# Sliding-window attention with a gated feed-forward: token tiles of 512 instead of 384 from the fifth tile on

## Chip, cores and metric

The kernel runs on one core of a Trainium2 chip. The metric is the time of one execution on the device, in microseconds (us). The median of three runs of the kernel before is given, and one further execution was profiled.

## What is computed

Attention over a window of 64 positions, causal, for 8 batches of 8 heads, 576 positions and 64 values a head; the heads' outputs side by side are the 512 features of 4608 tokens, and these go through a feed-forward layer with a ReLU gate (width 1536).

```python
scores = scale * np.matmul(q, k.transpose(0, 1, 3, 2))
rel = pos[:, None] - pos[None, :]
mask = (rel >= 0) & (rel < window)            # window = 64
attn = softmax(np.where(mask, scores, -1e9))
x = np.matmul(attn, v)      # (B, H, S, D) -> (B * S, H * D)
gate = np.maximum(x @ w_gate, 0.0)
out = gate * (x @ w_val) @ w_out
```

Inputs and output are fp32; the kernel computes in fp16 with fp32 accumulation.

## The kernel before, in words

Tokens are worked on in 12 tiles of `TT` = 384. A tile is two units of `U` = 192 tokens, and a unit is three windows of 64 queries; a batch has nine windows, or three units. For each tile there are two kinds of work.

Attention, by unit. The *scores* (`u_st`, L246) of four heads run beside each other in the four 32-row groups of TensorE, each head group into a bank of its own: 48 small matmuls, two pairs of banks of the pool `a_ps` (tag "a", two buffers of two banks). ScalarE takes the exponential bank by bank (`u_exp`, L257), VectorE multiplies by the band mask (`u_mask`, L265). The *values* (`u_pv`, L271) are 48 small matmuls, four beside each other by column groups, into one pair of banks; every query's sum of weights comes out as a 65th column. VectorE takes its reciprocal, multiplies (`u_recip`, `u_norm`) and transposes by 32x32 blocks into the feed-forward's input `xt` (`u_turn`, L315).

Feed-forward, by tile. `hidden` (L352): for each of 12 blocks of 128 features four matmuls with `w_gate` and four with `w_val`, each group into a bank of the pool `f_ps` (tag "h", four buffers of one bank); ScalarE writes the ReLU of the first to `r_sb`, VectorE multiplies it with the second into `g_sb` (L370). `output` (L410): for each 128 tokens 12 matmuls of 512 columns, a copy by ScalarE to `o_sb` (three buffers) and a store by the SyncE queue. The last block of the last tile (`output_last`, L419) is done in two column halves; the copy of the second half is split between ScalarE and VectorE, both into one `o_sb`.

The order on every engine is the order of the program, which is made when the kernel is built by a `Weaver` (L18): a heap of actions with due times and a clock in us that is advanced by an assumed cost for each group of matmuls. An action is put into the program when the clock has passed its time. `pair(t, TA, TB, P)` (L526) puts down the two score bursts, exponentials, masks, value bursts and transposes of tile t so that they fall into the feed-forward of tile t-1; `loads(t, T)` (L538) does the same for the loads of a batch's queries and keys, their transposes on VectorE (`qk_trans`, L175), and the values, which are loaded by the GpSimd queue (`v_load`, L182) and copied to the other half of the partitions by GpSimd (`v_spread`, L189). Before the loop over tiles all of this is put down at once, with T stepping by 25.4 from tile to tile:

```python
        T = 67.0
        for t in range(3, NU // 2):
            loads(t, T + 3.0)
            pair(t, T + 11.0, T + 14.0, T + 17.5)
            T += 25.4
```

`ready(n)` (L348) takes actions from the heap until the n-th unit has been transposed. The first two tiles have a schedule of their own.

Of the kernel before, what the change touches and what calls it, by code (L numbers as in the profile page):

```python
# [10 lines left out]
FP32 = mybir.dt.float32  # L11
FP16 = mybir.dt.float16
# [32 lines left out]
def kernel(  # L45
# [10 lines left out]
    nc = tc.nc  # L56
# [9 lines left out]
    G = 4  # L66
    scale = 1.0 / float(D) ** 0.5
    TT = 2 * U
    assert NT % TT == 0 and TT % 128 == 0

    consts = ctx.enter_context(tc.tile_pool(name="consts", bufs=1))
    persist = ctx.enter_context(tc.tile_pool(name="persist", bufs=1))
# [56 lines left out]

    def xt_tile(t):  # L130
        if t not in xts:
            xts[t] = x_sb.tile([128, NC, TT], FP16, name="xt")
        return xts[t]


# [46 lines left out]
    def v_load(u, parts=None):  # L182

        b, uu = divmod(u, UB)
        for g, lo, hi in parts or (((1, 0, 128), (3, 0, 128)), ((5, 0, 128),), ((7, 0, 128), (NG - 1, 64, 128)))[uu]:
            nc.gpsimd.dma_start(v16s[b % 2][lo:hi, g, :, 0:64],  # L186
                                v[b, :, 64 * g - 64 + lo:64 * g - 64 + hi].rearrange("h p d -> p h d"))

    def v_spread(u, copy=None, h0=0, h1=H):  # L189

        b, uu = divmod(u, UB)
        t = v16s[b % 2]
        copy = copy or nc.vector.tensor_copy
        for g0, g1 in (((0, 3),), ((4, 5),), ((6, 7),))[uu]:
            copy(t[64:128, g0:g1:2, h0:h1, 0:64], t[0:64, g0 + 1:g1 + 1:2, h0:h1, 0:64])  # L195
        for g0, g1 in (((2, 3),), ((4, 5),), ((6, 9),))[uu]:
            copy(t[0:64, g0:g1:2, h0:h1, 0:64], t[64:128, g0 - 1:g1 - 1:2, h0:h1, 0:64])  # L197
# [11 lines left out]
    def one_bank(name):  # L209
        return f_ps.tile([128, 512], FP32, name=name, tag="h")  # L210

    def two_banks(name):
        return a_ps.tile([128, 2, 512], FP32, name=name, tag="a")
# [10 lines left out]
    def st_block(to, g, hh, n, biased=False):  # L224

        b, w = divmod(n, NG)
        rows = slice(32 * g, 32 * g + 32)
        return [lambda dh=dh: nc.tensor.matmul(  # L228
            to, kTs[b % 2][rows, hh, 64 * w:64 * w + 128, dh], qTs[b % 2][rows, hh, 64 * w:64 * w + 64, dh],
            start=(dh == 0 and not biased), stop=(dh == 1), skip_group_check=biased) for dh in range(2)]  # L230

    def run_rows(rows):

        for step in zip(*rows):
            for dh in range(2):
                for block in step:
                    block[dh]()
# [77 lines left out]
    def u_turn(u, hhs=(0, 1)):  # L315

        d = units[u]
        c0 = U * (u % 2)
        h0, h1 = hhs[0], hhs[-1] + 1
        for hh in range(h0, h1):  # L320
            dst = xt_tile(u // 2)[:, 2 * hh:2 * hh + 2, c0:c0 + U].rearrange("p e (s c) -> p s e c", c=32)
            nc.vector.transpose(dst, d["x"][:, hh])  # L322
        if h1 == 2:
            del units[u]
            normed[0] = u + 1

    def plan_batch(b, load, trans):
        for i, (name, hh) in enumerate((n, hh) for n in "kq" for hh in range(2)):
            if load is not None:
                W.at(load, lambda name=name, hh=hh: qk_load(b, name, hh))  # L330
            W.at(trans[i], lambda name=name, hh=hh: qk_trans(b, name, hh))
# [16 lines left out]
    def ready(n):  # L348
        while normed[0] < n:
            W.pop()  # L350

    def hidden(t, spans, f0=0, f1=NF, each=1):  # L352

        if t not in gs:
            gs[t] = g_sb_p.tile([128, NF, TT], FP16, name="g_sb"), {}
        g_sb, done = gs[t]
        xt = xt_tile(t)
        n = spans[0][1] - spans[0][0]

        w = 512 // n  # L360
        each = max(each, w)

        def part(tile):
            return tile[:, 0:w * n].rearrange("p (w n) -> p w n", w=w)

        def relu(r_sb, h1):
            nc.scalar.activation(part(r_sb), part(h1), ACT.Relu)  # L367

        def gate(f, c0, r_sb, h2):
            nc.vector.tensor_tensor(g_sb[:, f:f + w, c0:c0 + n], part(r_sb), part(h2), MUL)  # L370
            done.update(dict.fromkeys(range(f, f + w), c0 + n))

        for fb in range(f0, f1, each):
            r_sbs = {}
            for i, wt in enumerate((wg, wv)):
                for c0, f in ((c0, f) for c0, _ in spans for f in range(fb, fb + each, w)):
                    h = f_ps.tile([128, 512], FP32, name=f"h{i}", tag="h")
                    for b in range(w):
                        W.advance(W.clock)
                        w_need(wt, f + b)  # L380
                        for c in range(NC):
                            nc.tensor.matmul(h[:, b * n:b * n + n], wt[:, c, (f + b) * 128:(f + b) * 128 + 128],  # L382
                                             xt[:, c, c0:c0 + n], start=(c == 0), stop=(c == NC - 1))
                        W.clock += 4 * (n + 7) / 2400.0
                    if i == 0:
                        r_sb = r_sbs[c0, f] = f_sb.tile([128, TT], FP32, name="r_sb", bufs=6)
                        W.at(W.clock, lambda r_sb=r_sb, h=h: relu(r_sb, h))
                    else:
                        W.at(W.clock, lambda f=f, c0=c0, r_sb=r_sbs[c0, f], h=h: gate(f, c0, r_sb, h))
# [10 lines left out]
    def out_evac(t, op, sub):  # L400
        def evac():
            o_sb = f_sb.tile([128, DM], FP32, name="o_sb")
            nc.scalar.copy(o_sb, op)  # L403
            nc.sync.dma_start(out[bass.ds(t * TT + sub * 128, 128)], o_sb)
        W.at(W.clock, evac)

    def op_tile():
        return f_ps.tile([128, DM], FP32, name="op", tag="h")

    def output(t, subs=range(TT // 128)):  # L410
        for sub in subs:
            op = op_tile()
            for f in range(NF):
                if f % 4 == 0:
                    W.advance(W.clock)
                out_mm(t, op, sub, f)
            out_evac(t, op, sub)

    def output_last(t):  # L419

        last = TT // 128 - 1
        output(t, range(last))
        W.drain()
        for col in range(2):
            op = op_tile()
            for f in range(NF):
                g_sb, _ = gs[t]
                nc.tensor.matmul(op[:, 0:256], g_sb[:, f, bass.ds(last * 128, 128)], wo[:, f, 256 * col:256 * col + 256],  # L428
                                 start=(f == 0), stop=(f == NF - 1))
            parts = ((0, 256, nc.scalar.copy, nc.sync),) if col == 0 else (  # L430
                (0, 128, nc.scalar.copy, nc.scalar), (128, 256, nc.vector.tensor_copy, nc.sync))
            o_sb = f_sb.tile([128, DM], FP32, name="o_sb")
            for c0, c1, copy, queue in parts:
                copy(o_sb[:, c0:c1], op[:, c0:c1])  # L434
                queue.dma_start(out[bass.ds(t * TT + last * 128, 128), 256 * col + c0:256 * col + c1], o_sb[:, c0:c1])

    def output_by_rows(t):
        ops = [op_tile() for _ in range(TT // 128)]
# [8 lines left out]
    with tc.manual_schedule():  # L447
# [78 lines left out]
        def pair(t, TA, TB, P):  # L526
            for u, T in ((2 * t, TA), (2 * t + 1, TB)):
                W.at(T, lambda u=u: u_st(u))
                plan_exps(T, u)
            W.at(P, lambda: u_pv(2 * t) + u_pv(2 * t + 1))  # L530
            for n in range(2):
                u = 2 * t + n
                W.at(P + 0.7 + 1.7 * n, lambda u=u: u_recip(u))
                for hh in range(2):
                    W.at(P + 0.9 + 0.5 * hh + 1.7 * n, lambda u=u, hh=hh: u_norm(u, hh))
                W.at(P + 1.9 + 1.7 * n, lambda u=u: u_turn(u))

        def loads(t, T):  # L538
            for u in (2 * t, 2 * t + 1):
                b, uu = divmod(u, UB)  # L540
                if uu == 0:
                    plan_batch(b, T - 12.0, (T, T + 1.4, T + 2.8, T + 4.2))
                W.at(T - 6.0, lambda u=u: v_load(u))
                W.at(T + 1.0, lambda u=u: v_spread(u, pool))

        for u in (4, 5):
            W.at(52.0, lambda u=u: v_spread(u, pool))
        pair(2, 56.0, 59.0, 62.5)
        T = 67.0
        for t in range(3, NU // 2):  # L550
            loads(t, T + 3.0)
            pair(t, T + 11.0, T + 14.0, T + 17.5)
            T += 25.4
        W.advance(15.3)
        hidden(0, ((0, U), (U, TT)), 0, 4, 4)
        hidden(0, ((0, TT),), 4, NF, 4)
        hidden(1, ((0, U),), each=4)
        output_by_rows(0)
        ready(4)
        hidden(1, ((U, TT),))  # L560
        output(1)
        for t in range(2, NU // 2):
            ready(2 * t + 2)
            hidden(t, ((0, TT),))
            (output if t < NU // 2 - 1 else output_last)(t)
        W.drain()


# [28 lines left out]
```

The softmax here doesn't subtract the row's maximum and nothing guards it: scores larger than these inputs give would overflow.

## Time and profile before

| | |
|---|---|
| median of 3 runs | 326.93 us (326.75 to 329.27) |
| the profiled execution | 326.75 us, span in the profile 325.1 us |
| mean granted TensorE clock | 0.989 |
| TensorE matmuls | 4043 recorded |
| hidden part of tile 2 (the third) begins | 67.81 |
| of tile 3 | 93.40 |
| of tile 4 | 118.99 |
| of tile 11 (the last) | 298.37 |
| last matmul ends | 321.78 |

The beginnings are read from the chain of waits in order of time, at the first hidden matmuls behind a tile's output matmuls. PE is TensorE's matmuls, PEld its weight loads, ACT is ScalarE, DVE VectorE, POOL GpSimd, SP SyncE. "L382" is line 382 of the kernel. In a list of groups `h<-xt,wg` names the tile written and those read; in brackets behind an instruction stand the engine's idle time before it and what ended it.

### The profile page before, as it was taken

The page shows a single profiled execution, that of the slowest core. Times are in us where ns is not written, and L with a number is a line of the kernel's source. Part 1 is how long each engine was busy: PE and PEld are TensorE (multiplying, and loading weights), DVE is VectorE, ACT ScalarE, POOL GpSimd, SP SyncE. Part 2 cuts the span into 40 slices and gives each one's busy share as a digit, 9 for nine tenths or more (in the row PEclk, how much of TensorE's full clock was granted, in tenths as well). Part 3 has the DMA queues.
Part 4 walks back from the last instruction along what each step waited for, and adds up shares of the span by engine and source line. Part 5 has one row for each costly group of instructions (what it writes and reads, how often), then busy time and mean ns, then how long its engine had stood idle before and what let it go on. Part 6 is the DMA issues. An engine that isn't in the chain of part 4 may idle for free.

```text
span 325.1 us, 9418 instructions
## 1 busy us (share of the span) xinstructions
PE 315.2 (97%) x4043; PEld 187.2 (58%) x4043; DVE 195.3 (60%) x406; ACT 132.0 (41%) x289; POOL 93.5 (29%) x138
## 2 busy tenths in 40 slices
PE   5699999999999999999999999999999999999995
PEld 2586949555556556645646645655655655564653
DVE  5937963687937824739648653685694681571430
ACT  3443324535334433623613713713623632543321
POOL 8666335284835300166052030065000000000000
PEclk9599999999999999999999999999999999999999
DMA  8999998989798960087495571038002002002002
GB/s 216 184 184 209 195 113 163 165 143 127 51 208 83 157 123 0 5 105 121 77 115 95 86 85 56 2 50 107 2 21 80 3 2 97 2 2 99 1 0 98
DMA packets 52490, 29.51 MB, mean 91 GB/s; under 512 B 38880, under 2 KB 43872, under 8 KB 52448
## 3 DMA queue, kind: packets, MB, share of 16 engines
q0 software_dynamic: 46688, 18.29, 48.2%
q1 hardware_dynamic: 5616, 10.55, 8.9%
q8 instruction: 31, 0.51, 0.6%
q14 instruction: 11, 0.09, 0.1%
q10 hardware_dynamic: 144, 0.07, 0.1%
HBM read 37.75 MB, written 9.44 MB: 145 GB/s over the span
## 4 chain that ended last, share of the span: by engine, by line
PE 95%; DMA 2%; POOL 2%; issue 0%; DVE 0%; ACT 0%; POOLq 0%; ACTq 0%
PE h L382 59%; PE op L396 28%; PE pv L288 3%; PE st L228 3%; DMA v<-in_v_dram 2%; PE op L428 1%; POOL v L186 1%; POOL k L162 0%; POOL v L197 0%; POOL v L195 0%; POOL q L162 0%; PE st L202 0%; POOL ident L102 0%; POOL ident L106 0%; DVE o_sb L434 0%
## 5 line engine op out<-in xcount | busy, mean ns | idle before, releaser
L370 DVE TENSOR_TENSOR g_sb<-r_sb,h 128x384 f16<-128x384 f32 x144 | 78.5, 548 | 92.4 <-PE h L382 91.7
L382 PE MATMUL h<-xt,wg 128*128 128x384 f16 (+1 forms) x640 | 116.6, 312 | 0.0
L382 PE MATMUL h<-xt,wv 128*128 128x384 f16 (+1 forms) x640 | 115.5, 310 | 0.0
L367 ACT ACTIVATE r_sb<-h 128x384 f32<-128x384 f32 x144 | 70.8, 494 | 86.3 <-PE h L382 46.0
L396 PE MATMUL op<-wo,g_sb 128*128 128x512 f16 x420 | 93.3, 379 | 0.0
L382 PEld LDWEIGHTS <-wg 128*128 128x128 f16 x640 | 60.4, 99 | 34.0 <-DVE xt L322 0.2
L382 PEld LDWEIGHTS <-wv 128*128 128x128 f16 x640 | 59.7, 98 | 32.0
L396 PEld LDWEIGHTS <-g_sb 128*128 128x128 f16 x420 | 40.5, 98 | 47.1
L186 POOL DMA_DIRECT2D v<-in_v_dram x41 | 34.4, 855 | 71.3 <-PE pv L288 68.5
L403 ACT COPY o_sb<-op 128x512 f32<-128x512 f32 x35 | 20.5, 585 | 82.8 <-PE op L396 82.6
L262 ACT ACTIVATE p<-st 128x384 f16<-128x384 f32 (+1 forms) x104 | 41.5, 478 | 15.2 <-PE st L228 14.8
L267 DVE TENSOR_TENSOR p<-p,mask 128x384 f16<-128x384 f16 x88 | 30.9, 367 | 15.6 <-ACT p L262 15.0
L195 POOL COPY v<-v 64x512 f16<-64x512 f16 (+1 forms) x21 | 15.5, 738 | 48.1 <-DMA v<-in_v_dram 47.7
L312 DVE TENSOR_TENSOR x<-pv,r 128x384 f16<-128x384 f32 x48 | 24.8, 552 | 0.9
L322 DVE STREAM_TRANSPOSE xt<-x 128x384 f16<-128x384 f16 x48 | 24.6, 551 | 0.0
L180 DVE STREAM_TRANSPOSE kT<-k 128x576 f32<-128x576 f32 x16 | 19.8, 1236 | 0.2 <-ACT k L173 0.2
L180 DVE STREAM_TRANSPOSE qT<-q 128x576 f32<-128x576 f32 x16 | 19.6, 1228 | 0.1
L228 PEld LDWEIGHTS <-kT 32*128 32x128 f16 x1152 | 11.1, 94 | 10.8 <-issue 8.7
L228 PE MATMUL st<-qT,kT 32*128 32x64 f16 x1152 | 13.8, 191 | 3.6 <-DVE qT L180 3.6
L197 POOL COPY v<-v 64x512 f16<-64x512 f16 (+1 forms) x21 | 15.8, 754 | 1.0
L288 PEld LDWEIGHTS <-p 128*32 128x32 f16 x1152 | 11.5, 97 | 5.0 <-issue 3.5
L288 PE MATMUL pv<-v,p 128*32 128x65 f16 x1152 | 13.2, 199 | 0.6 <-POOL v L197 0.5
(39 smaller groups left out, 56.1 us busy)
## 6 DMA issues: line engine op xcount, KB each, us to landing
out_dram<-o_sb SPq DMA_DIRECT2D x35, 256.0 KB, 2.0
k<-in_k_dram POOLq DMA_DIRECT2D x15, 288.0 KB, 5.4
q<-in_q_dram POOLq DMA_DIRECT2D x15, 288.0 KB, 7.0
v<-in_v_dram POOLq DMA_DIRECT2D x31, 128.0 KB, 6.1
wg<-in_moe_w_gate_dram POOLq DMA_DIRECT2D x6, 256.0 KB, 6.7
wv<-in_moe_w_val_dram POOLq DMA_DIRECT2D x6, 256.0 KB, 8.2
wo<-in_moe_w_out_dram POOLq DMA_DIRECT2D x3, 512.0 KB, 12.1
v<-in_v_dram POOLq DMA_DIRECT2D x10, 64.0 KB, 5.7
```

The costliest lines, as they stand in the source:

```text
L180: nc.vector.transpose(dst.rearrange("p (i j) -> p j i", i=32)[:, j0:j1], src[:, j0:j1])
L186: nc.gpsimd.dma_start(v16s[b % 2][lo:hi, g, :, 0:64], v[b, :, 64 * g - 64 + lo:64 * g - 64 + hi].rearrange("h p d -> p h d"))
L228: return [lambda dh=dh: nc.tensor.matmul(to, kTs[b % 2][rows, hh, 64 * w:64 * w + 128, dh], qTs[b % 2][rows, hh, 64 * w:64 * w + 64, dh], ...
L262: nc.scalar.activation(d["p"][i][:, UB * h0:UB * h1].rearrange("p n c -> p (n c)"), d["st"][i][:, U * h0:U * h1], ACT.Exp, scale=scale)
L267: nc.vector.tensor_tensor(p, p, mask[:, None, :].to_broadcast([128, p.shape[1], 64]), MUL)
L288: nc.tensor.matmul(to[32 * j:32 * j + 32, c:c + D + 1], p_of(u, G * hh + j, w)[:, 32 * s:32 * s + 32], v16s[b % 2][:, vw, G * hh + j, 0:D ...
L312: nc.vector.tensor_tensor(d["x"][:, hh], pv_of(d, u, hh)[:, :, 0:D].rearrange("p s (c e) -> p s e c", e=2), d["r"][:, hh, :, :, None].to_b ...
L322: nc.vector.transpose(dst, d["x"][:, hh])
L367: nc.scalar.activation(part(r_sb), part(h1), ACT.Relu)
L370: nc.vector.tensor_tensor(g_sb[:, f:f + w, c0:c0 + n], part(r_sb), part(h2), MUL)
L382: nc.tensor.matmul(h[:, b * n:b * n + n], wt[:, c, (f + b) * 128:(f + b) * 128 + 128], xt[:, c, c0:c0 + n], start=(c == 0), stop=(c == NC ...
L396: nc.tensor.matmul(op, g_sb[:, f, bass.ds(sub * 128, 128)], wo[:, f], start=(f == 0), stop=(f == NF - 1))
```

## The change

The first four tiles keep 384 tokens; the remaining 3072 tokens become six tiles of 512. `xt`, `g_sb` and `r_sb` are as wide as that for all tiles.

A wide tile has eight windows, two *quads* of four. The scores of a quad fill four banks wholly, 512 columns each (two head halves of four windows), 64 matmuls; exponentials and masks are of 512 columns. The values of the whole tile are one burst of 128 matmuls into five banks: for each half of the heads a pair of banks (seven blocks of 32 queries each), and one single bank from the feed-forward's pool for the last two blocks of both halves. Reciprocals and norms are by bank, three for each half, the single bank first, and the transpose is by half.

The attention of the next tile is put down when a tile's feed-forward begins, from the clock at that point, and the loads with it for the tile after the next; a batch's three value loads now come together. `output_last` gives each of its three copies an `o_sb` of its own.

```diff
+    WT = 512
+    NS = 4
+    NL = (NT - NS * TT) // WT
+    starts = [TT * t for t in range(NS)] + [NS * TT + WT * t for t in range(NL)]
+    widths = [TT] * NS + [WT] * NL
...
-            xts[t] = x_sb.tile([128, NC, TT], FP16, name="xt")
+            xts[t] = x_sb.tile([128, NC, WT], FP16, name="xt")
...
+    def q_st(qd):
+
+        halves = [two_banks("st") for _ in range(2)]
+        d = quads[qd] = {"st": [halves[g // 2][:, g % 2] for g in range(G)], "p": [None] * G}
+        run_rows([[st_block(d["st"][g][:, 256 * hh + 64 * i:256 * hh + 64 * i + 64], g, hh, q_window(qd, i))
+                   for hh in range(2) for i in range(QW)] for g in range(G)])
+        return 0.72
...
+    def t_pv(t):
+
+        d = wides[t] = {"pv": [two_banks("pv") for _ in range(2)], "rest": one_bank("pv"),
...
+        for qh in range(2):
+            qd = 2 * (t - NS) + qh
+            for hh in range(2):
+                for i in range(QW):
+                    b, vw = divmod(q_window(qd, i), NG)
+                    for s in range(2):
+                        n = 2 * (QW * qh + i) + s
+                        to = d["pv"][hh][:, n // BS, VW * (n % BS):] if n < 2 * BS else d["rest"][:, VW * (2 * hh + n - 2 * BS):]
+                        for j in range(G):
+                            nc.tensor.matmul(to[32 * j:32 * j + 32, 0:D + 1],
...
+    def plan_wide(t, TA, TB, P):
+        for qd, T in ((2 * (t - NS), TA), (2 * (t - NS) + 1, TB)):
+            W.at(T, lambda qd=qd: q_st(qd))
+            for g in range(G):
+                W.at(T + 0.8 + 0.55 * g, lambda qd=qd, g=g: q_exp(qd, g))
+                W.at(T + 1.35 + 0.55 * g, lambda qd=qd, g=g: q_mask(qd, g))
+        W.at(P, lambda: t_pv(t))
+        for hh in range(2):
+            W.at(P + 0.7 + 3.0 * hh, lambda hh=hh: t_recip(t, hh))
+            for i, k in enumerate((2, 0, 1)):
+                W.at(P + 1.0 + 3.0 * hh + 0.5 * i, lambda hh=hh, k=k: t_norm(t, hh, k))
+            W.at(P + 2.4 + 3.0 * hh, lambda hh=hh: t_turn(t, hh))
...
-            o_sb = f_sb.tile([128, DM], FP32, name="o_sb")
             for c0, c1, copy, queue in parts:
+                o_sb = f_sb.tile([128, DM], FP32, name="o_sb")
                 copy(o_sb[:, c0:c1], op[:, c0:c1])
...
+        def wide_loads(t, T):
...
+            if w0 <= NG * b:
+                plan_batch(b, T - 12.0, (T, T + 1.4, T + 2.8, T + 4.2))
+            for u in us:
+                W.at(T - 6.0, lambda u=u: v_load(u))
+                W.at(T + 1.0, lambda u=u: v_spread(u, pool))
+
+        def ahead(t):
+            T = W.clock
+            if t + 1 < NS:
+                pair(t + 1, T + 11.0, T + 14.0, T + 17.5)
+            elif t + 1 == NS:
+                plan_wide(t + 1, T + 9.5, T + 13.0, T + 16.2)
+            elif t + 1 < NS + NL:
+                plan_wide(t + 1, T + 12.0, T + 17.0, T + 22.5)
+            if NS <= t + 2 < NS + NL:
+                wide_loads(t + 2, T + 36.5 if t >= NS else T + 28.5)
...
-        for t in range(2, NU // 2):
-            ready(2 * t + 2)
-            hidden(t, ((0, TT),))
-            (output if t < NU // 2 - 1 else output_last)(t)
+        for t in range(2, NS + NL):
+            ready(t)
+            ahead(t)
+            hidden(t, ((0, widths[t]),))
+            (output if t < NS + NL - 1 else output_last)(t)
```

More of the change, by code (lines that the diff above doesn't have):

```diff
@@ L68 @@
     TT = 2 * U
-    assert NT % TT == 0 and TT % 128 == 0
+    WT = 512
+    NS = 4
+    NL = (NT - NS * TT) // WT
+    assert NT == NS * TT + NL * WT and TT % 128 == 0
+    starts = [TT * t for t in range(NS)] + [NS * TT + WT * t for t in range(NL)]
+    widths = [TT] * NS + [WT] * NL
     consts = ctx.enter_context(tc.tile_pool(name="consts", bufs=1))
@@ L324, in u_turn, with q_window @@
             del units[u]
-            normed[0] = u + 1
+            normed[0] = (u + 1) // 2 - 1
+    QW = 4
+    WS = 2 * WT // 64
+    BS = 512 // VW
+    quads = {}
+    wides = {}
+    def q_window(qd, i):
+        return NS * TT // 64 + QW * qd + i
+    def q_st(qd):
[4 more added lines that the diff above has]
+        return 0.72
@@ new lines, in q_exp, with q_mask @@
+    def q_exp(qd, g):
+        d = quads[qd]
+        d["p"][g] = a_p.tile([128, 2 * QW, 64], FP16, name="pw")
+        nc.scalar.activation(d["p"][g].rearrange("p n c -> p (n c)"), d["st"][g], ACT.Exp, scale=scale)
+    def q_mask(qd, g):
+        p = quads[qd]["p"][g]
+        nc.vector.tensor_tensor(p, p, mask[:, None, :].to_broadcast([128, 2 * QW, 64]), MUL)
+    def t_pv(t):
+        d = wides[t] = {"pv": [two_banks("pv") for _ in range(2)], "rest": one_bank("pv"),
+                        "x": a_n.tile([128, 2, WS, 2, D // 2], FP16, name="xw"), "r": a_n.tile([128, 2, WS, 1], FP32, name="rw")}
+        for qh in range(2):
[8 more added lines that the diff above has]
+                            nc.tensor.matmul(to[32 * j:32 * j + 32, 0:D + 1],
+                                             quads[qd]["p"][j][:, QW * hh + i, 32 * s:32 * s + 32],
+                                             v16s[b % 2][:, vw, G * hh + j, 0:D + 1],
+                                             start=True, stop=True, skip_group_check=True)
+        return 1.25
@@ new lines, in t_parts, with t_recip, t_norm @@
+    def t_parts(d, hh):
+        rest = d["rest"][:, 0:4 * VW].rearrange("p (a s c) -> p a s c", a=2, c=VW)
+        return [(d["pv"][hh][:, k, 0:BS * VW].rearrange("p (s c) -> p s c", c=VW), BS * k, BS * k + BS) for k in range(2)] + [
+            (rest[:, hh], 2 * BS, WS)]
+    def t_recip(t, hh):
+        d = wides[t]
+        for pv, s0, s1 in t_parts(d, hh):
+            nc.vector.reciprocal(d["r"][:, hh, s0:s1], pv[:, :, D:D + 1])
+    def t_norm(t, hh, k):
+        d = wides[t]
+        pv, s0, s1 = t_parts(d, hh)[k]
+        nc.vector.tensor_tensor(d["x"][:, hh, s0:s1], pv[:, :, 0:D].rearrange("p s (c e) -> p s e c", e=2),
+                                d["r"][:, hh, s0:s1, :, None].to_broadcast([128, s1 - s0, 2, D // 2]), MUL)
@@ new lines, in t_turn @@
+    def t_turn(t, hh):
+        dst = xt_tile(t)[:, 2 * hh:2 * hh + 2].rearrange("p e (s c) -> p s e c", c=32)
+        nc.vector.transpose(dst, wides[t]["x"][:, hh])
+        if hh == 1:
+            normed[0] = t
+    def plan_wide(t, TA, TB, P):
[10 more added lines that the diff above has]
+            W.at(P + 2.4 + 3.0 * hh, lambda hh=hh: t_turn(t, hh))
@@ L354, in hidden @@
         if t not in gs:
-            gs[t] = g_sb_p.tile([128, NF, TT], FP16, name="g_sb"), {}
+            gs[t] = g_sb_p.tile([128, NF, WT], FP16, name="g_sb"), {}
         g_sb, done = gs[t]
@@ L385, in hidden @@
                     if i == 0:
-                        r_sb = r_sbs[c0, f] = f_sb.tile([128, TT], FP32, name="r_sb", bufs=6)
+                        r_sb = r_sbs[c0, f] = f_sb.tile([128, WT], FP32, name="r_sb", bufs=6)
                         W.at(W.clock, lambda r_sb=r_sb, h=h: relu(r_sb, h))
@@ L403, in evac @@
             nc.scalar.copy(o_sb, op)
-            nc.sync.dma_start(out[bass.ds(t * TT + sub * 128, 128)], o_sb)
+            nc.sync.dma_start(out[bass.ds(starts[t] + sub * 128, 128)], o_sb)
         W.at(W.clock, evac)
@@ L408, in op_tile, with output @@
         return f_ps.tile([128, DM], FP32, name="op", tag="h")
-    def output(t, subs=range(TT // 128)):
-        for sub in subs:
+    def output(t, subs=None):
+        for sub in range(widths[t] // 128) if subs is None else subs:
             op = op_tile()
@@ L419, in output_last @@
     def output_last(t):
-        last = TT // 128 - 1
+        last = widths[t] // 128 - 1
         output(t, range(last))
@@ L431, in output_last @@
                 (0, 128, nc.scalar.copy, nc.scalar), (128, 256, nc.vector.tensor_copy, nc.sync))
-            o_sb = f_sb.tile([128, DM], FP32, name="o_sb")
             for c0, c1, copy, queue in parts:
+                o_sb = f_sb.tile([128, DM], FP32, name="o_sb")
                 copy(o_sb[:, c0:c1], op[:, c0:c1])
-                queue.dma_start(out[bass.ds(t * TT + last * 128, 128), 256 * col + c0:256 * col + c1], o_sb[:, c0:c1])
+                queue.dma_start(out[bass.ds(starts[t] + last * 128, 128), 256 * col + c0:256 * col + c1], o_sb[:, c0:c1])
     def output_by_rows(t):
@@ L548 @@
         pair(2, 56.0, 59.0, 62.5)
+        def wide_loads(t, T):
+            w0 = q_window(2 * (t - NS), 0)
+            b = (w0 + 2 * QW - 1) // NG
+            us = list(range(UB * b, UB * b + UB)) if w0 <= NG * b else []
+            if t == NS:
+                us.insert(0, UB * b - 1)
+            if w0 <= NG * b:
[13 more added lines that the diff above has]
+                wide_loads(t + 2, T + 36.5 if t >= NS else T + 28.5)
+        W.at(15.0, lambda: loads(3, 70.0))
         T = 67.0
[L550 to L553, printed above, removed]
         W.advance(15.3)
@@ L558 @@
         output_by_rows(0)
-        ready(4)
+        ready(1)
         hidden(1, ((U, TT),))
         output(1)
-        for t in range(2, NU // 2):
-            ready(2 * t + 2)
-            hidden(t, ((0, TT),))
-            (output if t < NU // 2 - 1 else output_last)(t)
+        for t in range(2, NS + NL):
[3 more added lines that the diff above has]
+            (output if t < NS + NL - 1 else output_last)(t)
         W.drain()
```

## The prediction, made before the changed kernel ran

> **What bounds the kernel now.** I read the page's busy shares first, then the waits of TensorE (PE), the chain of waits, and the windows of each tile. The busy shares and the chain:
>
> ```profile
> PE 315.2 (97%) x4043; PEld 187.2 (58%) x4043; DVE 195.3 (60%) x406; ACT 132.0 (41%) x289; POOL 93.5 (29%) x138
> PE 95%; DMA 2%; POOL 2%; issue 0%; DVE 0%; ACT 0%; POOLq 0%; ACTq 0%
> ```
>
> PE is on the chain for 95% of the span. A busy PE is not yet a PE at its peak, so I ask what it waited for (engine, operation, releaser: us in total, times, longest):
>
> ```profile
> PE st L228 <- DVE qT L180: 3.6, 2, 2.0
> PE st L202 <- DVE zero L461: 2.3, 1, 2.3
> PE pv L288 <- POOL v L197: 0.5, 1, 0.5
> ```
>
> All three lie in the start-up, which the change leaves alone. One period of a 384-token tile follows from the chain in order of time (start, us, what); x counts recorded matmuls, and some records are missing (a score burst has 48, a value burst 96):
>
> ```profile
> 144.72 9.75 PE h L382 x60
> 154.47 0.48 PE st L228 x39
> 154.95 2.71 PE h L382 x16
> 157.66 0.48 PE st L228 x47
> 158.14 2.71 PE h L382 x16
> 160.85 0.94 PE pv L288 x80
> 161.79 0.76 PE h L382 x4
> 162.54 7.77 PE op L396 x36
> ```
>
> 60 hidden matmuls take 9.75, so 0.1625 us each; 36 output matmuls take 7.77, 0.2158 each; score and value matmuls come to 0.010 each. Groups of 16 behind a burst take 2.71 where 16 x 0.1625 = 2.60: each burst costs 0.11 beyond its own time. The period is 96 x 0.1625 + 7.77 + 2 x 0.48 + 0.94 = 25.27, plus 3 x 0.11 = 0.32: 25.59. The windows of single tiles say the same:
>
> ```profile
> 118.99:144.72 25.73, 25.73 (x327) 14.53 (x324) 13.27 (x30) 10.81 (x23) 6.56 (x8) 1.00 0.19 33
> 144.72:170.31 25.59, 25.59 (x325) 14.46 (x324) 16.77 (x34) 10.70 (x23) 10.36 (x15) 1.00 0.78 111
> 247.08:272.78 25.70, 25.70 (x326) 14.51 (x324) 16.09 (x33) 10.70 (x23) 0.00 (x0) 1.00 0.09 33
> ```
>
> (stretch, length, then busy us of PE, PEld, DVE, ACT, POOL, granted clock, DMA share, GB/s.) Two periods are 0.12 longer: there only 12 hidden matmuls stand between the score bursts, and the second burst is held until ScalarE (ACT) has read the last bank:
>
> ```profile
> 129.94 1.25 ACT L262 ACTIVATE p<-st 128x384 f16<-128x384 f32 x3 [0.67 <-PE st L228]
> 131.06 0.51 ACT L367 ACTIVATE r_sb<-h 128x384 f32<-128x384 f32 x1
> 131.43 0.53 ACT L262 ACTIVATE p<-st 128x384 f16<-128x384 f32 x1
> ```
>
> The last exponential ends at 131.96; the chain has that burst last 0.62 instead of 0.48. So PE has no idle time worth removing from the fifth tile on: what can be won is fixed cost per matmul and per burst.
>
> **What the Trainium skill says.** "TensorE: Matmul & The Clock Gate", section "Wait — 56ns, not 53.3ns?": a warm matmul takes its columns at 2.4 GHz plus a fixed 2.5 ns or so. The trace agrees: 384 columns, 160.0 + 2.5 = 162.5 ns; 512 columns, 213.3 + 2.5 = 215.8. "PSUM — Partial Sum Buffer", section "Specifications (TRN2)": eight banks of 512 fp32 values a partition; the program is held to that (four banks in pairs, four single), and 512 columns fill a bank. "SBUF — State Buffer", section "Terms": VectorE (DVE) and GpSimd (POOL) share a port pair, locked for a whole instruction. The trace agrees: two masks took 1.75 us beside a POOL copy, where 1.12 was three elsewhere.
>
> ```profile
> 79.09 1.03 POOL L195 COPY v<-v 64x1024 f16<-64x1024 f16 x1 [0.30 <-DMA v<-in_v_dram]
> 79.27 1.75 DVE L267 TENSOR_TENSOR p<-p,mask 128x384 f16<-128x384 f16 x2 [0.41 <-ACT p L262]
> ```
>
> **The change part by part.**
>
> *Hidden and output matmuls.* Per 512 tokens 128 hidden matmuls at 0.1625 (20.80) become 96 at 0.2158 (20.72), the rate that the output matmuls of the same width already show: 0.08 won, over six wide tiles 0.50. Output matmuls per token stay.
>
> *Bursts.* The number of score and value matmuls per token stays, with the same packing by four; a wide score burst has 64 (0.64), a value burst 128 (1.25). Tiles five to twelve become six wide ones, so two periods with their three bursts fall away: 2 x 0.32 = 0.64 at 0.11 a burst. Unknown is whether the 0.11 stays for a value burst that now stands between output matmuls; bounds 0 and 0.2, I keep 0.11. The two waits of 0.12 go (0.14 and 0.11, 0.25), as the wide schedule has 20 hidden matmuls, 4.32 + 0.11 = 4.43 us, between the bursts.
>
> *Check by sums.* A wide period is 20.72 + 10.36 + 1.28 + 1.25 + 0.32 = 33.93. Tile four (from 93.40), which carries the first wide attention, goes from 25.59 to 25.59 + 0.32 + 0.31 = 26.22. Five wide periods are 169.65; the last, without attention, is 20.72 + 7.77 + 2.63 (the two half-width columns, as now) = 31.12. PE would end at 93.40 + 26.22 + 169.65 + 31.12 = 320.39, against 321.78: 1.39, as 0.50 + 0.64 + 0.25.
>
> *Last copies.* Both copies of the last column share one tile, and DVE's starts only when ACT's is done:
>
> ```profile
> 321.85 0.27 ACT L434 COPY o_sb<-op 128x128 f32<-128x128 f32 x1 [0.98 <-PE op L428]
> 322.14 0.37 ACTq L435 DMA_DIRECT2D out_dram<-o_sb  x1
> 322.14 0.29 DVE L434 COPY o_sb<-op 128x128 f32<-128x128 f32 x1 [7.52 <-ACT o_sb L434]
> ```
>
> With tiles apart it can start at 321.86: 0.28 won, if the buffer is free. Three buffers rotate, so DVE's is that of the third row block, whose DMA is issued where 319.80 stands now and lands 2.0 later, at 321.8: just in time. Bounds 0 and 0.29; I take 0.28.
>
> *Exponentials and masks.* From the forms of 192 (361 ns) and 384 columns (499 ns) an exponential of 512 is about 0.59 and starts 0.47 after the one before ((1.25 - 0.50) / 2 = 0.38, plus 128 x 0.72 ns). In a wide tile the order is two, a relu, two: first start 0.14 after the burst, last end about 2.6. The next score burst comes at 4.43, so 1.8 us to spare. Behind the second burst the last mask (367 ns at 384, at most 0.49) ends by 3.0-3.5; the values come at 4.43 + 0.43 = 4.86. In tile four the gaps are still 16 narrow matmuls (2.71) against an exponential ending about 2.5 and a mask at 3.0, needed by the second half of the value burst at 3.33. Here 0 to 0.8 can be lost once; I take 0.1.
>
> *Five banks for values.* The values hold both pairs and one single bank. The single one comes free once the second half's short norm is done. A half costs DVE three reciprocals (0.6), norms (1024 columns at 552/384 ns = 1.47) and a transpose (1.47), 3.54; the first half is written 0.94 into the burst, so the bank is free at 0.94 + 3.54 + 0.6 + 0.28, about 5.4 after its start. With four rotating banks, three groups come in between: in a wide tile three output blocks, the next user at 1.25 + 46 x 0.2158 = 11.2; in tile four one hidden group and two blocks, at 7.1. Hidden. The transposed values are ready at 0.94 + 7.1 = 8.0 and needed at 11.2 (tile four: about 8.7, with a gate in the queue, against 9.7). Hidden too, by the output matmuls.
>
> *DVE and ACT in sum.* Scaled by columns, a wide period asks DVE for 12 gates (0.73), 8 masks (0.49), values 7.1 and 4 input transposes (1.23): 8.8 + 3.9 + 7.1 + 4.9 = 24.7 of 33.9. ACT: 12 relus (0.59), 8 exponentials (0.59), 4 copies (0.585), 14.1. Four input transposes between gates already ran beside narrow groups with no PE idle; wide groups give 1.73 a gate instead of 1.30.
>
> *Loads.* All three parts of a batch's values are now loaded and spread together. SP's queue only takes output stores, now four a tile. On POOL, ahead of tile four, three more value loads are issued before the copies that stood before them, from about 72 instead of 80.76; POOL runs some 20 us ahead of the values' use, so no burst waits for it. But the copies may then stand beside the fourth tile's masks (82 to 85), and a locked mask can delay its value burst: 0 to 0.6, I take 0.2. Later value loads wait for the value burst, land about 6 later, and their copies (six of 0.6 to 1.0) run beside norms and gates, long before the next burst 34 us on.
>
> Sum: 1.39 + 0.28 - 0.1 - 0.2 = 1.37. The profiled execution took 326.75 with a span of 325.1; the span becomes 323.7. The median, 326.93, lies 0.18 above it: 326.93 - 1.37, about 325.5.
>
> **The rivals.**
>
> *Nothing gained (0.20).* The lost time beside a burst grows with its columns and not with its number, so the 0.64 is not won, and both one-time waits cost near their ends (1.1 instead of 0.3): 1.37 - 0.64 - 0.8, about 0: 326.9. For it: the 0.11 is only a remainder of a sum. Against: it is the same behind score bursts in every period.
>
> *Slower: the quad's chain on ACT (0.10).* Exponentials of 512 columns queue with wider relus, and the next burst waits for them. Twelve quads share the gain of 1.67, so it turns to a loss once each holds PE by 0.14, a chain of 4.6 where I reckon 2.6. At 0.3 each: 326.93 + 3.6 - 1.7 = 328.9. For it: the wait of 0.12 seen now is this one. Against: 1.8 us to spare, and ACT under half busy.
>
> *More than forecast (0.08).* The value burst between output matmuls costs nothing extra (0.5) and no one-time wait appears (0.3): 324.7.
>
> **How the numbers follow.** The forecast, 325.5, has 0.62 and an own range of 325.0 to 326.2. The range of 8 in 10, 324.6 to 327.4, takes in the first and third rival and leaves out most of the slower one. About 1% can be told from no change here, so faster means under 323.7 and slower over 330.2. Neither is reached by a case's middle: faster 0.03, same 0.92, slower 0.05 (the far end of the slower rival).
>
> **What would show it.** In the changed kernel: hidden groups of 512 columns at 0.2158 a matmul, wide windows of 33.9, PE's list of waits no longer than now, the tail copy on DVE beside ACT's. Wrong if wide windows exceed 34.1 (4/3 of 25.59), or if PE waits for an exponential, a mask or a norm in each of them.

## The result, and the profile after

The changed kernel takes 325.36 us, median of 6 runs (324.98 to 325.67); the kernel before, beside it, 327.12 (326.75 to 329.27). The ratio of the means is 0.9935, 95% interval 0.9907 to 0.9962: 0.65% shorter. (One execution of the kernel before, 329.27, weighs in that mean; the medians differ by 0.54%, and when the changed kernel was run again later the ratio was 0.9952, 0.9938 to 0.9965.) The profiled execution took 324.98 with a span of 323.3, against 326.75 and 325.1.

Busy shares and chain, from the page of the changed kernel:

```profile
PE 313.7 (97%) x3851; PEld 168.4 (52%) x3851; DVE 192.1 (59%) x370; ACT 127.0 (39%) x249; POOL 93.7 (29%) x138
...
PE 94%; DMA 2%; POOL 2%; issue 0%; ACT 0%; DVE 0%; DVEq 0%; POOLq 0%
```

PE is as busy as before, with the 192 hidden matmuls fewer that the wide tiles have (3851 for 4043). What it waited for:

```profile
PE st L233 <- DVE qT L185: 3.5, 2, 1.9
PE st L207 <- DVE zero L547: 2.3, 1, 2.3
```

Both lines lie in the start-up, as before. From the third tile on the list has no wait of PE. One wide period, from the chain in order of time (start, us, what):

```profile
153.44 12.09 PE h L468 x56
165.53 0.62 PE st L233 x55
166.14 4.42 PE h L468 x20
170.56 0.62 PE st L233 x61
171.18 4.42 PE h L468 x20
175.60 0.43 PE op L482 x2
176.03 1.23 PE pv L371 x120
177.27 10.04 PE op L482 x46
```

Fifty-six hidden matmuls take 12.09, 0.2159 each. The groups behind a burst take 4.42 where 20 x 0.2158 = 4.32, and the 46 output matmuls behind the value burst 10.04 where 9.93: 0.11 behind each burst, also between output matmuls. But the score burst of 64 takes 0.62 and the value burst of 128 takes 1.23, or 1.18 to 1.26 in the other tiles. (In these chain lines x leaves out some of a burst's small matmuls. The window of this tile below holds all of them: 96 + 48 + 128 + 128 = 400 of its 401.) The windows of the fourth tile, of the wide ones that follow (two of five shown) and of the last:

```profile
93.40:119.55 26.15, 26.15 (x390) 15.02 (x388) 18.66 (x38) 11.57 (x23) 8.62 (x13) 1.00 0.39 61
...
153.44:187.30 33.86, 33.86 (x401) 16.21 (x400) 21.13 (x38) 13.43 (x24) 10.75 (x15) 1.00 0.58 83
...
254.97:288.78 33.81, 33.81 (x401) 16.15 (x400) 16.97 (x34) 13.43 (x24) 0.00 (x0) 1.00 0.09 33
288.78:319.91 31.13, 31.11 (x156) 15.05 (x154) 8.26 (x12) 9.88 (x17) 0.00 (x0) 1.00 0.09 34
```

In both executions the third tile's hidden part begins at 67.81, so the two can be laid over each other: the last matmul ends at 319.91 instead of 321.78, 1.87 earlier. The span is only 1.8 shorter, so a little was given back behind the last matmul. There (instructions in order of time: start, us, engine):

```profile
317.91 0.33 SPq L490 DMA_DIRECT2D out_dram<-o_sb  x1
...
319.97 0.27 ACT L520 COPY o_sb<-op 128x128 f32<-128x128 f32 x1 [0.94 <-PE op L514]
...
320.34 0.29 DVE L520 COPY o_sb<-op 128x128 f32<-128x128 f32 x1 [10.05 <-ACT o_sb L520]
320.66 0.33 SPq L521 DMA_DIRECT2D out_dram<-o_sb  x1
```

VectorE's copy starts 0.43 behind the last matmul; before it was 0.36 (321.78 to 322.14). So 0.07 was given back, and the last copies won nothing. (The ends of matmuls are modelled, so that 0.02 more or less says nothing here.)

### The profile page after: what moved, and what is told of

It is laid out like the page before. It is cut to its first block, busy times and chain, and to the rows that moved or that the text cites. A ratio compares the mean times of both kernels' runs of the same rounds, so it can differ in the third digit from the quotient of the medians.

```text
span 323.3 us, 8901 instructions
## 1 busy us (share of the span) xinstructions
PE 313.7 (97%) x3851; PEld 168.4 (52%) x3851; DVE 192.1 (59%) x370; ACT 127.0 (39%) x249; POOL 93.7 (29%) x138
## 4 chain that ended last, share of the span: by engine, by line
PE 94%; DMA 2%; POOL 2%; issue 0%; ACT 0%; DVE 0%; DVEq 0%; POOLq 0%
PE h L468 59%; PE op L482 28%; PE st L233 3%; PE pv L371 2%; DMA v<-in_v_dram 2%; PE pv L293 1%; POOL v L191 1%; DMA out_dram<-o_sb 1%; POOL k L167 0%; POOL v L200 0%; POOL v L202 0%; ACT o_sb L489 0%; POOL q L167 0%; PE st L207 0%; POOL ident L107 0%
## 5 line engine op out<-in xcount | busy, mean ns | idle before, releaser
L456 DVE TENSOR_TENSOR g_sb<-r_sb,h 128x512 f16<-128x512 f32 (+1 forms) x120 | 75.4, 631 | 86.3 <-PE h L468 84.5
L468 PE MATMUL h<-xt,wg 128*128 128x512 f16 (+2 forms) x544 | 112.5, 338 | 0.1
L468 PE MATMUL h<-xt,wv 128*128 128x512 f16 (+2 forms) x544 | 111.3, 335 | 0.0
L453 ACT ACTIVATE r_sb<-h 128x512 f32<-128x512 f32 (+1 forms) x120 | 66.7, 558 | 89.5 <-PE h L468 80.4
L356 DVE TENSOR_TENSOR pw<-pw,mask 128x512 f16<-128x512 f16 x48 | 19.3, 422 | 14.6 <-ACT pw L352 14.3
L352 ACT ACTIVATE pw<-st 128x512 f16<-128x512 f32 x48 | 25.7, 605 | 5.0 <-PE st L233 4.5
L267 ACT ACTIVATE p<-st 128x384 f16<-128x384 f32 (+1 forms) x40 | 14.0, 441 | 8.2 <-PE st L233 8.2
L391 DVE TENSOR_TENSOR xw<-pv,rw 128x448 f16<-128x448 f32 (+1 forms) x36 | 16.2, 507 | 0.4
L396 DVE STREAM_TRANSPOSE xt<-xw 128x1024 f16<-128x1024 f16 x12 | 14.9, 1244 | 0.4
L272 DVE TENSOR_TENSOR p<-p,mask 128x384 f16<-128x384 f16 x24 | 9.5, 414 | 3.6 <-ACT p L267 3.5
```

Of the source, the lines that this page charges most:

```text
L352: nc.scalar.activation(d["p"][g].rearrange("p n c -> p (n c)"), d["st"][g], ACT.Exp, scale=scale)
L356: nc.vector.tensor_tensor(p, p, mask[:, None, :].to_broadcast([128, 2 * QW, 64]), MUL)
L391: nc.vector.tensor_tensor(d["x"][:, hh, s0:s1], pv[:, :, 0:D].rearrange("p s (c e) -> p s e c", e=2), d["r"][:, hh, s0:s1, :, None].to_bro ...
```

## The experiments

All are compared with the kernel before on their own chip; four were run together, then three, then three. The executions start their third tile between 67.8 and 68.6, so a step of some tenths is read from that point to the last matmul, or from the last matmul to the end of the span, and not from the spans alone.

### Fixed cost of a matmul

```diff
-            hidden(t, ((0, widths[t]),))
+            hidden(t, ((0, widths[t]),) if t < NS else ((0, WT // 2), (WT // 2, WT)))
```

> The changed kernel, with the hidden matmuls of the six wide tiles in two halves of 256 columns: 192 a tile instead of 96, same columns. Theory (2.5 ns fixed for each matmul beside its columns): 576 more matmuls x 2.5 ns = 1.44, span 324.8, a wide period 34.1. Rival (the time goes with the columns alone, and what the wide tiles won lies in the bursts only): span 323.3. Rival (weight loads of 99 ns do not keep up with matmuls of 109 ns): span above 326.

Measured: 326.29 us (325.78 to 328.24), ratio to the kernel before 0.9982 (0.9973 to 0.9990). A wide period of this kernel:

```profile
187.95:222.05 34.10, 34.10 (x498) 25.57 (x497) 20.99 (x38) 13.53 (x24) 8.77 (x12) 1.00 0.58 84
```

From the third tile (67.96) to the last matmul (321.53) it takes 253.57, the changed kernel 252.10: 1.47 for 576 more matmuls, 2.55 ns each. Both rivals fall: PEld is busy for 25.6 of a period instead of 16.2 and holds nothing up. The wide tiles have 192 hidden matmuls fewer than the narrow ones for the same tokens (768 to 576), so their share of the gain is 0.5.

### Fixed cost of a burst

```diff
-        W.at(P, lambda: t_pv(t))
+        W.at(P, lambda: t_pv(t, 0))
+        W.at(P + 1.4, lambda: t_pv(t, 1))
+        P += 0.8
```

`t_pv(t, qh)` does the matmuls of one quad, at half the cost assumed for the schedule; nothing else of it changes.

> The changed kernel, with the value burst of each wide tile in two bursts of 64, one for each quad, with three output matmuls (in the first wide tile four hidden ones) between them. Theory (each burst costs a fixed time, about 0.11 in the matmuls behind it and 0.08 to 0.1 at its own start): six more bursts, 6 x 0.2 = 1.2, span 324.5, wide period 34.05. Rival (lost time goes with a burst's columns): span 323.3.

Measured: 326.10 us (325.87 to 326.60), ratio 0.9975 (0.9965 to 0.9985). The chain of this kernel in one tile:

```profile
176.77 0.62 PE pv L373 x56
177.39 0.75 PE op L486 x3
178.15 0.65 PE pv L373 x56
178.79 9.39 PE op L486 x43
```

Two bursts of 64 take 0.62 and 0.65, and three output matmuls 0.75 instead of 0.65. From 68.29 to 321.31 are 253.02, 0.92 more than the changed kernel, 0.15 for each of six more bursts, a quarter less than the expected 0.2. The rival, that time goes with columns, falls. No run splits a score burst in the same way: its fixed cost is read from burst sizes and sums of periods further down.

### The wait of the next score burst

```diff
-                plan_wide(t + 1, T + 12.0, T + 17.0, T + 22.5)
+                plan_wide(t + 1, T + 12.0, T + 14.2, T + 22.5)
```

> The changed kernel, with the second score burst of five wide tiles placed 8 hidden matmuls behind the first instead of 20. In the changed kernel the last of four exponentials ends 2.65 behind the burst, with one relu among them. Theory (the next burst waits for the last exponential): 8 matmuls take 1.84, so each second burst waits about 0.75 (2.65 - 1.84, less if the relu falls behind); five tiles, 3 to 4, span 326.5 to 327. Rival (the waits seen in the kernel before had another cause): span 323.3.

Measured: 329.68 us (329.36 to 330.04), ratio 1.0082 (1.0067 to 1.0097), with a span of 328.0: slower than both expectations. PE's list of waits gains a line, and in one tile one sees how it comes about:

```profile
PE st L233 <- ACT pw L352: 3.5, 5, 0.7
```

```profile
168.37 0.61 ACT L453 ACTIVATE r_sb<-h 128x512 f32<-128x512 f32 x1
168.85 1.11 ACT L352 ACTIVATE pw<-st 128x512 f16<-128x512 f32 x2
169.11 0.20 PE L233 MATMUL st<-qT,kT 32*128 32x64 f16 x2
...
170.01 0.67 PE L233 MATMUL st<-qT,kT 32*128 32x64 f16 x62 [0.70 <-ACT pw L352]
```

Two matmuls of the burst go at 169.11, into banks already read; the third stands until the last exponential has ended at 169.96. That is 0.90 lost, in five tiles 4.5, of which the list shows 0.70 each because the two matmuls count as busy. To the last matmul the kernel takes 4.43 more. From the end of the first burst (167.34) to that of the last exponential are 2.6, as the changed kernel has it (166.14 to 168.76). With 20 matmuls between, 4.42, some 1.8 are to spare: the slower rival of the prediction is a real mechanism that the changed kernel's due times keep away from.

### The two longer periods of the kernel before

```diff
-            pair(t, T + 11.0, T + 14.0, T + 17.5)
+            pair(t, T + 10.2, T + 14.0, T + 17.5)
```

> The kernel before, with the first score burst of tiles four to twelve due 0.8 earlier, so that 16 to 20 hidden matmuls stand between the two bursts everywhere. Theory: the two waits of 0.12 (periods of 25.73 and 25.70) are gone, all periods 25.59, span 324.85, 0.25 below the kernel before. Rival (those periods were longer for another reason): span 325.1.

Measured: 326.58 us (326.48 to 327.32), ratio 0.9991 (0.9983 to 1.0000): 0.3 us at the edge of what the runs resolve. The profile is clear; the two windows that were 25.73 and 25.70:

```profile
119.54:145.13 25.59, 25.59 (x326) 14.46 (x324) 13.20 (x30) 10.81 (x23) 6.56 (x8) 1.00 0.19 32
247.50:273.06 25.56, 25.56 (x325) 14.43 (x324) 16.00 (x33) 10.70 (x23) 0.00 (x0) 1.00 0.09 33
```

From 68.36 to 322.05 are 253.69, 0.28 less than the kernel before. The span itself, 325.3, is no shorter, as the start-up was 0.55 longer in this execution. So 0.28 of the change's 1.87 could be had with narrow tiles, by due times alone.

### The last copies

Three kernels made from the changed one, and the changed one again. With buffers that nothing else uses:

```diff
-                o_sb = f_sb.tile([128, DM], FP32, name="o_sb")
+                o_sb = f_sb.tile([128, DM], FP32, name=f"o_last{col}{c0}", bufs=1)
```

> The changed kernel, with a buffer for each of the last three copies that nothing else uses. In the changed kernel the last matmul ends at 319.91, ScalarE's copy starts at 319.97, VectorE's at 320.34. Theory A (the two copies read the same PSUM bank and are ordered for that; the change only swapped the shared SBUF tile for a wait on the third block's store, landed at 319.92): VectorE's copy starts at the end of ScalarE's, 0.29 after it, 0.08 earlier than in the changed kernel; span 323.2. Rival B (the prediction's: it was the shared SBUF tile, and the late store took its place): both copies start together, 0.37 earlier; span 322.9.

With the copies back in one tile (the change's three lines taken back):

> The changed kernel, with the last copies put back into one tile. Theory A: VectorE's copy starts 0.29 after ScalarE's, no late store is waited for; span 323.2, 0.1 shorter than the changed kernel's 323.3. Rival B (tiles apart win 0.28): span 323.6.

And with the last 256 columns in two PSUM banks:

```diff
-        for col in range(2):
+        for c0, n, copy, queue in ((0, 256, nc.scalar.copy, nc.sync), (256, 128, nc.scalar.copy, nc.scalar), (384, 128, nc.vector.tensor_copy, nc.sync)):
             op = op_tile()
...
+            o_sb = f_sb.tile([128, DM], FP32, name=f"o_last{c0}", bufs=1)
+            copy(o_sb[:, 0:n], op[:, 0:n])
+            queue.dma_start(out[bass.ds(starts[t] + last * 128, 128), c0:c0 + n], o_sb[:, 0:n])
```

> The changed kernel, with the last 256 columns as two groups of 128 in PSUM banks of their own, and buffers of their own; ScalarE copies the first, VectorE the second, queues as before. Theory A (VectorE's copy was held by ScalarE's reading of the same bank): VectorE's copy starts 0.06 behind the last matmul instead of 0.33 to 0.43, SyncE's last store is issued 0.3 earlier against the last matmul, and the span ends 3.05 behind the last matmul instead of 3.39; 24 matmuls of 128 columns at 57 ns are 1.37 instead of 1.31. Net about 0.3 shorter than the changed kernel. Rival (the end follows the store issued by ScalarE's queue, 2.6 to 2.8 behind its issue in all kernels so far): the end stays 3.3 behind the last matmul.

Buffers of their own, then banks of their own (two kernels):

```profile
320.35 0.27 ACT L520 COPY o_last<-op 128x128 f32<-128x128 f32 x1 [0.94 <-PE op L514]
...
320.65 0.29 DVE L520 COPY o_last<-op 128x128 f32<-128x128 f32 x1 [9.93 <-ACT o_last L520]
```

```profile
320.01 0.27 ACT L517 COPY o_last<-op 128x128 f32<-128x128 f32 x1 [0.30 <-PE op L514]
...
320.68 0.29 DVE L517 COPY o_last<-op 128x128 f32<-128x128 f32 x1 [9.66 <-PE op L514]
```

With buffers apart VectorE still waits for ScalarE, though nothing is shared any more but the tile `op` in PSUM, which both read. With banks apart its copy is released by PE, 0.02 behind the last matmul (320.66). That start alone would prove little, as ScalarE's copy had ended at 320.28 there. But in the trace VectorE's copy waits for ScalarE's semaphore in own_buffers and for PE's alone in own_banks: the order between the two copies is gone from the program. So the bank that both read is enough to hold VectorE's copy. Whether the order goes by the bank or by the tile that fills it, and whether a shared SBUF tile alone would hold the copy too, no run tells. The changed kernel's further 0.08 is the store of the third row block, in whose buffer VectorE writes. Its chain of waits shows the store land at 319.92, and four semaphore waits of 0.05, each with 0.05 between (the first and the last are shown):

```profile
317.91 2.01 DMA out_dram<-o_sb
...
319.95 0.05 DVEq L520
...
320.25 0.05 DVEq L520
...
320.34 0.29 DVE o_sb L520
```

| kernel | us (range of 5 runs) | ratio to the kernel before | VectorE's copy behind the last matmul | end of the span behind it |
|---|---|---|---|---|
| own_buffers | 324.89 (324.86 to 325.26) | 0.9941 (0.9927 to 0.9954) | 0.33 | 3.3 |
| joined_copies | 324.99 (324.93 to 325.16) | 0.9943 (0.9931 to 0.9956) | 0.37 | 3.3 |
| changed_again | 325.48 (324.97 to 325.65) | 0.9952 (0.9938 to 0.9965) | 0.43 | 3.4 |
| own_banks | 324.81 (324.62 to 325.29) | 0.9934 (0.9922 to 0.9947) | 0.02 | 2.9 |

The last two stand on one chip. 

> The changed kernel once more, so that the next two stand beside it on one chip. From the last matmul's end to the span's end 3.39, as before; VectorE's last copy 0.43 behind the last matmul.

Separating banks takes about 0.4 off the end in the trace (0.34 were expected), and 0.67 off the median; as the intervals of the two ratios overlap, the times alone don't show a gain. own_banks has the lowest median of the kernels tried, level with one_last_copy below; own_buffers and joined_copies can't be told from them by their ratios.

Cutting the last block into 384 and 128 columns, one copy each, has the same aim:

```diff
-        for col in range(2):
+        for c0, n, queue in ((0, 384, nc.sync), (384, 128, nc.scalar)):
...
```

> The changed kernel, with the last block's columns cut into 384 and 128 instead of 256 and 256, one ScalarE copy each, with buffers of their own. Theory A: only one copy of 128 columns and one store follow the last matmul; the last store is issued about 0.36 after it instead of 0.75; the matmuls are 12 x 162.5 + 12 x about 60 ns = 2.67 instead of 2.63; span 322.95. Rival: the end is set by what follows the stores and not by their issue: span 323.3.

Measured: 325.46 us (325.13 to 325.90), ratio 0.9956 (0.9944 to 0.9969). The last store is issued 0.33 behind the last matmul (319.96) as hoped, but the span, 323.5, ends about 3.6 behind it (the expectation below has 3.54, from a rounded span): the expectation failed.

```profile
320.29 0.37 ACTq L518 DMA_DIRECT2D out_dram<-o_last  x1
```

The store now goes by ScalarE's queue, so I tried VectorE and SyncE's queue for it:

> As narrow_end (384 and 128 columns), but the last copy on VectorE and its store on SyncE's queue, so that none of the last stores goes by ScalarE's queue. narrow_end ended 3.54 behind its last matmul, although its last store was issued 0.35 earlier than the changed kernel's; in the kernels that end on SyncE's store the span ends 2.3 behind the end of that issue, in narrow_end 2.84 behind the end of ScalarE's. Theory (ScalarE's queue costs about 0.5 more at the end): last issue ends 0.7 behind the last matmul, span 3.0 behind it, 0.4 shorter than the changed kernel. Rival (a fixed end not set by the last store): 3.3 or more.

Measured: 324.81 us (324.78 to 325.42), ratio 0.9937 (0.9925 to 0.9950), end about 3.2 behind the last matmul. This lies between the two expectations of 3.0 and 3.3.

The traces show what the time between the last issue and the end of the span is made of. The last store lands 1.7 behind the start of its issue in all of these kernels, by either queue:

```profile
out_dram<-o_sb SPq DMA_DIRECT2D x1, 64.0 KB, 1.7
```

Then SyncE's closing instructions have to follow. In the changed kernel the store lands at 322.33, SyncE's first DRAIN begins at 322.4 and the span ends at 323.3, 0.9 behind the landing; own_buffers and own_banks have the same 0.9. In one_last_copy 1.1 pass behind the landing, in narrow_end 1.5: there the store lands at 322.0 and the DRAIN begins only at 322.6. So an earlier last store was not followed at once. Why the DRAIN comes so late in narrow_end stays open.

## Why the prediction was right

The time, 325.5 forecast and 325.36 measured, came out closer than its parts, and that closeness is luck. The forecast fall was 1.37, the spans fell by 1.8. To the last matmul PE gained 0.78 more than reckoned; the last copies, 0.28 in the forecast, lost 0.07, which hides 0.35 of it. And the forecast was taken off a median of 326.93, which became 327.12 with more runs. The main mechanism, fixed costs of PE, was right; one step of it was too small, and one side step had the wrong cause.

- *That PE's fixed costs are all there is to win*: right. No wait was left to remove but the two of 0.12, and none came in. The sum to the last matmul was 1.39 less 0.3; it is 1.87.
- *Matmuls, 0.50*: right; 2.55 ns for each of 576 more in half_width_hidden.
- *The two waits, 0.25*: right; 0.28 in before_gap_20.
- *Bursts, 0.64*: too small, and this is the step that was mis-sized. It counted only the 0.11 behind a burst and scaled the burst itself by its matmuls (64 as 0.64, 128 as 1.25). A score burst went from 0.48 to 0.62 for 16 more matmuls, 8.5 ns each, so about 0.07 of it does not scale; the value burst, from 0.94 to about 1.22 for 32 more, has about 0.1. In sums: a narrow period spends 25.59 - 15.60 - 7.77 = 2.22 on its bursts, a wide one 33.86 - 20.72 - 10.36 = 2.78 and the fourth tile 26.15 - 23.37 = 2.78; eight times 2.22 less six times 2.78 is 1.08, or 0.18 for each of six bursts less. two_value_bursts adds them singly at 0.15. With 0.50 and 0.25 that makes 1.83 of the 1.87. Four of the six are score bursts; that one of those costs about 0.18 is read from the burst sizes and these sums alone.
- *One-time losses, 0.1 and 0.2*: neither came. The fourth tile took 26.15, less than the 26.22 without a loss. The second loss was in part luck: the POOL copies did stand beside the fourth tile's masks, and one mask was held past the copy's end (83.93). The last mask ended at 85.41, 0.7 later than before (84.70). The new due times had put the value burst 0.65 later too, at 85.45 instead of 84.80, which the prediction had not reckoned with, so nothing was lost. The copy and the masks:

```profile
82.89 1.04 POOL L202 COPY v<-v 64x1024 f16<-64x1024 f16 x1
...
83.11 1.03 DVE L272 TENSOR_TENSOR p<-p,mask 128x384 f16<-128x384 f16 x1 [0.27 <-ACT p L267]
...
84.53 0.88 DVE L272 TENSOR_TENSOR p<-p,mask 128x384 f16<-128x384 f16 x3
```

- *Last copies, 0.28*: wrong, -0.07. The step read the releaser "ACT o_sb" as the shared SBUF tile; without that tile (own_buffers) the wait was still there, and it went with the PSUM bank that both copies read (own_banks). In the Trainium skill "PSUM — Partial Sum Buffer", section "Terms", calls two engines on the same partitions of one bank at once an error, reads included. That would be a reason for the order; no run here lets them collide. The buffer, reckoned just in time, came 0.08 late, through the waits behind the landing.
- *Five banks, ACT's and DVE's sums*: right in kind. DVE was asked for 21.1 of a wide period (24.7 reckoned), ACT for 13.4 (14.1); PE waited for neither.
- *Missing records*: a misreading without effect. The prediction took the low counts in the chain for missing records; the window of that period (144.72 to 170.31) counts 325, and a period has 324. Its sums go by the times of the bursts, which are right.
- *The rivals*: "nothing gained" fell with the fixed cost of a burst, which is larger than forecast. "More than forecast" was right in that no one-time wait appeared, and wrong in that a value burst between output matmuls would cost nothing extra (10.04 where 9.93). The slower rival turned up once its due time was moved, at 0.90 a burst; only the second burst of a tile waited, so its sum over twelve quads counted about twice as many bursts as can wait.

## What to carry to other kernels

Where one engine is busy throughout and waits for nothing, count its switches: a change of tile size is worth (matmuls less) x (fixed cost of one) plus (bursts less) x (fixed cost of one), and the second is read from two burst sizes, not by dividing one. Before two engines are to copy in parallel, look at what both of them read as well as at what they write. And before moving bursts closer, measure the chain that frees their banks; here the chain took 2.6 us: a gap of 4.42 cost nothing, one of 1.8 cost 0.9 us a tile.

## What the runs showed of the hardware

- In the changed kernel a wait of VectorE on the stores before it was worked off in four steps of 0.1, so the copy starts 0.42 behind the landing of the last store (319.92 to 320.34).
- Packed by four, a small matmul of a score or value burst adds 8.5 to 8.8 ns to it (0.48 to 0.62 for 16 more, 0.94 to 1.22 for 32 more), less than the 10 that dividing a burst by its matmuls suggests.
- Behind the start of the last store's issue come 1.7 us until it lands and 0.9 more to the end of the span, where a store by SyncE is last and one by ScalarE goes before it (the changed kernel, own_buffers, own_banks). With both last stores by SyncE (one_last_copy) 1.1 follow the landing, with ScalarE's as the last (narrow_end) 1.5.
